# Retention's decays earlier on GpSimd, block-end copies behind the cosine chain, one input split moved

## The chip, the cores and the metric

One core of one Trainium2 chip runs the whole program. The metric is the device time of one execution in microseconds (us); the time before is the median of three runs.

## What is computed

Retention (a linear attention with a decay per head) over 4 batches, 8 heads, 576 positions and 64 channels, then two feed-forward layers of 2304 tokens with 512 inputs and 2048 hidden columns. All inputs are fp32.

```python
scores = scale * np.matmul(q, k.transpose(0, 1, 3, 2))
ret = scores * Dmat          # Dmat[i, j] = gamma[h] ** (i - j) for i >= j, else 0
x = np.matmul(ret, v)        # to [2304, 512]
h = x @ w_in;  g = h * np.cos(h);  x = g @ w_out
h = x @ w_in2; g = piecewise(h);   return g @ w_out2   # 0, (h + 1)**2 / 4 or h
```

## The kernel before, in words

Each fp32 product is made as three TensorE products of a rounded high part and a low remainder (high by high, high by low, low by high). So every activation has a high part (`gh`, made by ScalarE, ACT) and a low part (`gl`, made by GpSimd, POOL, as the difference of the value and its high part).

The first layer runs in "slots", 80 of them. A slot is one pair of a token block (256 tokens once, then four blocks of 512) and one of 16 hidden column groups. Slots 32 to 47, 48 to 63 and 64 to 79 are blocks 2, 3 and 4; the last slots of blocks 0 and 1 are 27 and 31. The program is written out slot by slot (the loop at line 1044), and from slot 24 on every engine keeps the order in which the steps are written. The steps of slot s have letters (line 653): `m` is the first product (12 matmuls into bank `h`, or into `bkS`/`bkO` in block 4), `a` and `A` round the phase (ACT, then DVE), `b` is the cosine (two ACT instructions, `t<-t`), `C` multiplies by h (DVE, `t<-t,h`), `g` and `G` make `gh` and `gl`, and `M` is the second product (12 matmuls into the four banks `bky0` to `bky3`), which is issued two slots later (`LAG`). One slot of the loop from slot 28 on writes, in this order: `C`, `g`, `G` of the slot before; the plan of half slot 2s; `m`; some conversion work; `a`, `A`; the plan of half slot 2s + 1; `M` of slot s - 2; `evac`; conversion work on DVE; `b`; conversion work on ACT.

"Conversion work" turns the second layer's weights, which arrive as 64-bit words, into fp32 pieces (`X`, `W`, `V`, `cw`, `tw`): a queue for DVE and one for ACT, from which the loop takes a budget per half slot (`drain`).

`evac` (line 600) copies the four `bky` banks to SBUF after a block's last second product: ACT takes banks 0 and 2, DVE banks 1 and 3 (`st`), and SyncE (SP) stores them. A block's last second product is issued in slots 29, 33, 49 and 65.

The retention for blocks 3 and 4 runs inside the slots of the block before, in nine chunks (numbers 11 to 19) of 64 or 128 tokens. Function `mk` (line 690) puts each chunk's steps at half slots: the load of q, k, v (`qkv`) at `gl_`, 5 to 9 half slots ahead; the decays on POOL, which multiply q (`qkv<-qkv,qtb`) and, save for a batch's last chunk, k (`qkv<-qkv,ktb`) by powers of gamma; at `pos[0]` the scores and the product with the carried state (TensorE into `bkO` and `bkS`) and the masking (`masked`, DVE, `R`); at `pos[1]` `attend`, the state products and the new state (`T`); at `pos[2]` `high` (ACT) and `low` (DVE), which read `bkO` and `bkS` into the next block's input `xhl`. Chunks 14 and 19 end a batch and have no k decay. The scores of the next chunk use the same two banks, so they also wait for `low`.

The second layer's program comes from a list of operations with positions, which `listed` (line 1318) sorts. Its inputs are split into high and low by `split_q` (line 888): seven splits, of which those in `EARLY` are written at the end of the first layer and the others, with their positions in `XEARLY`, in the list. Each is a copy on ACT (`xc<-q`) and a difference on DVE. The first product of the second layer fills bank `bkT0`; `seed`, an ACT copy `bkT<-bkT`, puts it into `bkT1`, where the next product (of `PRODS` index 2) adds to it.

Nearly all instructions carry line 128, a helper's, so places are told by tile names and times.

Of the kernel before, what the change touches and what calls it, by code (L numbers as in the profile page):

```python
# [23 lines left out]
NC = DFF // P  # L24
# [10 lines left out]
NKB = NQ // 2  # L35
NX = 9
SPOS = (-44, -42)
EARLY = (0, 2, 3, 1, 4)
XEARLY = {5: 6, 6: 8}
T0 = 28.0  # L40
ORDER = "1 5 6 2 7 G 4 3".split()
FIRST = "1 L0 6 L1 2 5 7 N 4 3".split()
# [9 lines left out]
LAG = 2  # L52
# [58 lines left out]
def retention_moe_kernel(ctx: ExitStack, tc: tile.TileContext, qk, kv, win1, wout1, win2, wout2, ktab, out):  # L111
# [25 lines left out]
    V, A, G, SY, PE = [Ordered(e) for e in (nc.vector, nc.scalar, nc.gpsimd, nc.sync, nc.tensor)]  # L137
# [117 lines left out]
    def begin(L, i, c, after=None):  # L255
        return Conversion(L, i, c, after).X()
# [3 lines left out]
    def home1(i, c):  # L260
        if i == 0:
            wi[0, c] = wr.tile([P, 2, DM], F32R, tag="wi", name="wi")
            return wi[0, c]
        wo[0, c] = wp.tile([P, 2, DM], F32R, tag=f"wo{c}", name=f"wo{c}")
        return wo[0, c]

    def store1(c):
        SY.dma_start(out=wd[c], in_=f(wi[0, c]))
# [6 lines left out]
    def load_wi(c):  # L275
        t = wr.tile([P, 2, DM], F32R, tag="wi", name="wi")
        SY.dma_start(out=f(t), in_=wd[c])
        wi[0, c] = t

    xhl = {}  # L280
    CH = {}
# [269 lines left out]
    slots = []  # L551
# [42 lines left out]
    def copy_out(e, t, y, scale):  # L594
        if e % 2 == 0:
            A.activation(t, y, AF.Copy, scale=scale)
        else:
            V.tensor_scalar(out=t, in0=y, scalar1=scale, scalar2=None, op0=ALU.mult)

    def evac(s, home=None, only=None):  # L600
        l, c = slots[s]
        if c != NC - 1:
            return
        o, n = BLOCKS[l]
        per = 512 // n
        for e, y in enumerate(yb[l]):
            if only not in (None, e):
                continue
            t = stp.tile([P, 512], F32, tag="st", name="st") if home is None else home
            copy_out(e, t, y, -TWOPI)  # L610
            SY.dma_start(out=yd[:, e * per:(e + 1) * per, o:o + n], in_=t.rearrange("p (k n) -> p k n", k=per))
# [44 lines left out]
    def steps_of(s, which):  # L656
        for x in which:
            if (x, s) not in taken:
                taken.add((x, s))
                STEPS[x](s)  # L660
# [3 lines left out]
    def at(pos, fn):  # L664
        plan.setdefault(pos, []).append(fn)

    def run_plan(pos):
        for fn in plan.pop(pos, []):
            fn()
# [9 lines left out]
    for l in range(3, NBLK):  # L679
        s0, s1 = window[l]  # L680
        span = 2 * (s1 - s0) / len(members[l])
        for k, i in enumerate(members[l]):
            g = int(2 * s0 + k * span)
            e = int(2 * s0 + (k + 1) * span) - 1
            e = max(e, g)
            pos = [g, g + (e - g) // 3, e]
            ends[i] = e
            gl_ = max(g - 9, ends.get(i - 2, -99))

            def mk(i=i, g=g, pos=pos, gl_=gl_):  # L690
                def ld():
                    CH[i] = Chunk(i)
                    CH[i].place_in()
                    CH[i].load(after=lastpe[0])

                def go(*names):
                    return lambda: [getattr(CH[i], n)() for n in names]
                at(gl_, ld)
                at(g - 1, lambda: CH[i].decay_q(G))
                if not CHUNKS[i][1] + CHUNKS[i][2] == S:  # L700
                    at(g - 1, lambda: CH[i].decay_k(G))
                at(pos[0], go("scores", "across", "masked"))
                at(pos[1], go("attend"))
                if not CHUNKS[i][1] + CHUNKS[i][2] == S:
                    at(pos[1], go("state"))
                at(pos[1], go("add_state"))
                at(pos[2], go("high", "low"))
                crowd[pos[0]] = crowd.get(pos[0], 0.0) + 0.3
                crowd[pos[2]] = crowd.get(pos[2], 0.0) + 0.85
            mk()  # L710
# [146 lines left out]
    def home_early(tag, shape, dt=F32):  # L857
        if not early_pool:
            opening.close()
            early_pool.append(ctx.enter_context(tc.tile_pool(name="ep", bufs=1, side="right", reuse_waits="tile")))  # L860
        return early_pool[0].tile([P, *shape], dt, tag=tag, name=tag)

    def xat(k):
        if k not in xplace:
            if k in EARLY[:2]:
                xplace[k] = home_early(f"xc{k}", (2, 2, TH), F32R)
# [12 lines left out]
    def sum_q(eng, pos, to, a, b, how):  # L879
        e = G if eng == "POOL" else V  # L880

        def run():
            if qa[to][1] is None:
                qa[to][1] = home_early(f"q{to}", (2, TH))
            e.tensor_tensor(out=qa[to][1], in0=qa[a][1], in1=qa[b][1], op=how)
        op(eng, "pool" if eng == "POOL" else "wide", pos, run, (qa[a][0], qa[b][0]), (qa[to][0],))

    def split_q(eng, pos, k, sb=0):
        p = PRODS[k][0]
        if p == 6:  # L890
            sum_q(eng, pos - 2, 0, 4, 0, ALU.subtract)
        if p == 3:
            sum_q(eng, pos - 2, 3, 3, 0, ALU.subtract)
        u = qa[{1: 0, 6: 0, 2: 3, 7: 1, 5: 4, 4: 2, 3: 3}[p]]
        x = (sb * 7 + k) % NX
        hi, lo = ("x", x, 0), ("x", x, 1)
        op("ACT", "copy", pos, lambda: A.activation(xat(x)[:, 0], u[1], AF.Copy), (u[0],), (hi,))
        op("DVE", "wide", pos + 0.8, lambda: V.tensor_tensor(out=xat(x)[:, 1], in0=u[1], in1=f(xat(x)[:, 0]), op=ALU.subtract), (u[0], hi), (lo,))
# [18 lines left out]
    sum_q("DVE", 0, 1, 0, 1, ALU.subtract)  # L917
    for k in EARLY:
        split_q("DVE", 0, k)
# [9 lines left out]
    def drain(eng, budget, most=1e9):  # L929
        q = todo2[eng]  # L930
        while q and (q[0][2] is None or q[0][2] in seen2) and q[0][0] <= budget + 0.15 and (eng != "DVE" or spent[0] < most):
            cost, fn, _, says = q.pop(0)
            fn()
            seen2.add(says)
            budget -= cost
            spent[0] += cost * (eng == "DVE")
# [3 lines left out]
    def raw_of(j):  # L940
        load_raw(1, *bg[j])
# [96 lines left out]
    def then_last():  # L1038
        if not todo2["DVE"] and not todo2["ACT"] and last_work:
            for n, (eng, cost, fn) in enumerate(last_work):  # L1040
                queue_up(eng, cost, fn, ("last", n - 1) if n else None, ("last", n))
            last_work.clear()

    for s in range(N1):
        l, c = slots[s]
        if s == 24:
            by_hand[0] = 0
        if s >= bg0:
            by_hand[0] = 1
            share = whole * (s + 1.5 - bg0) / (N1 - 3 - bg0)  # L1050
            if s == bg0:
                for j in range(3):
                    raw_of(j)
            then_last()
            steps_of(s - 1, "CgG")
            run_plan(2 * s)
            for c2 in reload.get(s, []):
                load_wi(c2)
            steps_of(s, "m")
            drain("ACT", 1.1)  # L1060
            drain("DVE", 2.3 - crowd.get(2 * s, 0.0), share)
            steps_of(s, "aA")
            drain("ACT", 0.65)
            run_plan(2 * s + 1)
            steps_of(s - LAG, "M")
            evac(s - LAG)
            drain("DVE", 1.5 - crowd.get(2 * s + 1, 0.0), share)
            steps_of(s, "b")
            drain("ACT", 0.65)
            if s == N1 - 12:  # L1070
                for _, _, fn in inputs_at:
                    fn()
            continue
        run_plan(2 * s)
        steps_of(s, "m")
        if s >= 1:
            steps_of(s - 1, "CgG")
        steps_of(s, "haA")

        todo = [x for x in jobs.get(s, []) if x not in opened]  # L1080
        begun = [begin(0, *x) for x in todo]
        for x in todo:
            begun.pop(0).rest(home1(*x))
            if queue:
                load_raw(0, *queue.pop(0))
        for x in todo:
            if x[0] == 0:
                store1(x[1])
        run_plan(2 * s + 1)
        if s >= LAG:  # L1090
            steps_of(s - LAG, "M")
            evac(s - LAG)
        steps_of(s, "b")
        for c2 in reload.get(s, []):
            load_wi(c2)
# [211 lines left out]
    for k in range(7):  # L1307
        if k not in EARLY:
            split_q("DVE", XEARLY[k], k)
    for n in range(NSB * NKB):  # L1310
# [150 lines left out]
```

## Time and profile before

| | us |
|---|---|
| median of 3 runs | 846.78 (846.37, 846.78, 851.21) |
| the profiled execution | 849.83 |
| its span, first to last instruction | 848.0 |
| TensorE busy | 814.7 (96%) |
| VectorE (DVE) busy | 642.5 (76%) |
| ScalarE (ACT) busy | 542.3 (64%) |
| GpSimd (POOL) busy | 145.3 (17%) |

The first layer ends near 490 us; the rest is the second layer. In the rows a timeline line gives start, duration, engine, line, operation, what it writes and reads, shapes and count; in brackets the idle time of the engine before it and what ended it. The name there is that of the semaphore which came last by the profile. PE is TensorE.

### The profile page before, as it was taken

To read this page: it belongs to the slowest core of one execution; us is meant where nothing else is said; L and a number is where in the kernel's file an instruction comes from. 1 tells how busy PE (TensorE), PEld (TensorE's weight loads), DVE (VectorE), ACT (ScalarE), POOL (GpSimd) and SP (SyncE) were. 2 spreads that over 40 slices of the span, in tenths; PEclk is the share of its full clock that TensorE was granted. 3 is DMA by queue.
4 is the path that set the end of the run, shared out by engine and by line. 5 is a ranking of instruction groups with operands and counts; after the bars stand their busy time and mean duration, and the time that the engine had idled before them with its cause. 6 is when DMAs were issued, how large, how long until landed. Compare 5 with 4: busy or idle time off the path is not lost.

```text
span 848.0 us, 14727 instructions
## 1 busy us (share of the span) xinstructions
PE 814.7 (96%) x5550; PEld 733.9 (87%) x5550; DVE 642.5 (76%) x941; ACT 542.3 (64%) x889; POOL 145.3 (17%) x115
## 2 busy tenths in 40 slices
PE   8999899978999999999999989999999999999997
PEld 5888788866778777778878889999999999999997
DVE  7888878886678776778877558789597776874776
ACT  4778788745356655556665559778648786566672
POOL 2333222232322332322332100000000000000000
PEclk9999999998999999999999999999999999999999
DMA  9996999688567978666976468988889878898883
GB/s 350 379 385 255 346 329 324 238 287 296 176 246 257 339 277 321 217 219 247 357 295 219 161 214 287 319 255 255 255 292 332 276 255 257 252 325 252 252 254 137
DMA packets 78007, 232.92 MB, mean 275 GB/s; under 512 B 8304, under 2 KB 15088, under 8 KB 77936
## 3 DMA queue, kind: packets, MB, share of 16 engines
q1 hardware_dynamic: 77936, 231.98, 78.6%
q8 instruction: 44, 0.72, 0.3%
q14 instruction: 27, 0.22, 0.1%
HBM read 184.76 MB, written 47.19 MB: 274 GB/s over the span
## 4 chain that ended last, share of the span: by engine, by line
PE 54%; DVE 11%; ACT 6%; DMA 2%; issue 2%; SPq 0%; DVEq 0%; ACTq 0%
PE bkT L128 41%; PE h L128 6%; PE bky L128 5%; ACT t L128 4%; DVE t L128 4%; DVE V L128 3%; DVE tw L128 1%; PE bkO L128 1%; DMA wi<-wd 1%; DVE X L128 1%; PE bkS L128 1%; ACT tw L128 1%; DVE cw L128 1%; DVE xc L128 1%; ACT xc L128 0%
## 5 line engine op out<-in xcount | busy, mean ns | idle before, releaser
L128 PE MATMUL h<-xhl,wi 128*128 128x512 f32 (+1 forms) x816 | 184.3, 376 | 6.0 <-ACT hs L128 2.8
L128 PE MATMUL bkT<-xc,w 128*128 128x384 f32 x1008 | 180.5, 337 | 2.8 <-ACT bkT L128 2.8
L128 PEld LDWEIGHTS bkT<-xc,w 128*128 128x128 f32 x1008 | 176.3, 189 | 3.6 <-ACT bkT L128 3.5
L128 PEld LDWEIGHTS h<-xhl,wi 128*128 128x128 f32 x816 | 144.8, 193 | 34.6 <-ACT hs L128 3.2
L128 PE MATMUL bkT<-gh,w 128*128 128x384 f32 x672 | 170.9, 335 | 0.3 <-ACT bkT L128 0.3
L128 PE MATMUL bky<-gh,wo 128*128 128x512 f32 x504 | 155.5, 395 | 0.0
L128 POOL TENSOR_TENSOR gl<-t,gh 128x512 fp32r<-128x512 f32 (+1 forms) x76 | 101.9, 1341 | 311.2 <-ACT gh L128 244.6
L128 ACT ACTIVATE t<-t 128x512 f32<-128x512 f32 (+1 forms) x152 | 89.4, 591 | 60.4 <-DVE t L128 58.3
L128 PEld LDWEIGHTS bkT<-gh,w 128*128 128x128 f32 x672 | 121.4, 188 | 0.6 <-ACT bkT L128 0.6
L128 PE MATMUL bkT<-gl,w 128*128 128x384 f32 x336 | 112.3, 334 | 0.0
L128 PEld LDWEIGHTS bky<-gh,wo 128*128 128x128 f32 x504 | 94.7, 191 | 19.9 <-issue 0.3
L128 PE MATMUL bky<-gl,wo 128*128 128x512 f32 x252 | 96.0, 391 | 0.0
L128 DVE SCALAR_TENSOR_TENSOR t<-t,h 128x512 f32<-128x512 f32 x88 | 60.1, 683 | 29.4 <-ACT t L128 29.3
L128 ACT ACTIVATE gh<-t 128x512 fp32r<-128x512 f32 (+1 forms) x76 | 44.9, 591 | 33.8 <-DVE t L128 33.7
L128 PEld LDWEIGHTS bkT<-gl,w 128*128 128x128 f32 x336 | 63.1, 188 | 0.0
L128 PEld LDWEIGHTS bky<-gl,wo 128*128 128x128 f32 x252 | 47.6, 189 | 10.2
L128 DVE TENSOR_TENSOR gl<-a,gh 128x768 fp32r<-128x768 f32 x48 | 45.1, 953 | 13.5 <-ACT gh L128 13.5
L128 DVE SCALAR_TENSOR_TENSOR a<-bkT,a 128x768 f32<-128x768 f32 x36 | 34.4, 955 | 23.5 <-ACT a L128 22.9
L128 DVE TENSOR_TENSOR a<-bkT,a 128x768 f32<-128x768 f32 (+1 forms) x46 | 43.0, 937 | 11.0 <-PE bkT L128 11.0
L128 ACT ACTIVATE t<-h 128x512 f32<-128x512 f32 x44 | 26.0, 591 | 38.9 <-PE h L128 38.7
L128 ACT ACTIVATE X<-raw 128x512 f32<-128x512 f32 x61 | 40.4, 664 | 11.4 <-DMA raw<-in_win_dram 7.3
L128 ACT ACTIVATE gh<-a 128x768 fp32r<-128x768 f32 x48 | 40.2, 838 | 9.0 <-PE bkT L128 8.4
(159 smaller groups left out, 1211.5 us busy)
## 6 DMA issues: line engine op xcount, KB each, us to landing
w<-wq SPq DMA_DIRECT2D x84, 512.0 KB, 4.5
w<-wv SPq DMA_DIRECT2D x84, 512.0 KB, 4.4
wi<-wd SPq DMA_DIRECT2D x48, 512.0 KB, 4.7
raw<-in_win_dram SPq DMA_DIRECT2D x32, 512.0 KB, 5.2
raw<-in_wout_dram SPq DMA_DIRECT2D x32, 512.0 KB, 5.2
qkv<-in_qk_dram SPq DMA_DIRECT2D x16, 512.0 KB, 6.4
qkv<-in_kv_dram SPq DMA_DIRECT2D x16, 512.0 KB, 7.9
wd<-wi SPq DMA_DIRECT2D x16, 512.0 KB, 6.0
```

Source lines behind the costliest of these rows:

```text
L128: ins = fn(*args, **kw)
```

## The change

Three edits. The decays of chunks 11 to 19 are written at half slot g - 3 instead of g - 1, where g is the half slot of the chunk's scores. In the slots in which a block's last second product is issued, `C` of the same slot is written directly after `b`, and `evac` after that; the ACT conversion work at the end of such a slot is left to the next one. The split with index 4 (of the fifth product) moves from the first layer's end into the second layer's list, at position 4.

```diff
-EARLY = (0, 2, 3, 1, 4)
-XEARLY = {5: 6, 6: 8}
+EARLY = (0, 2, 3, 1)
+XEARLY = {4: 4, 5: 6, 6: 8}
...
                 at(gl_, ld)
-                at(g - 1, lambda: CH[i].decay_q(G))
+                at(g - 3, lambda: CH[i].decay_q(G))
                 if not CHUNKS[i][1] + CHUNKS[i][2] == S:
-                    at(g - 1, lambda: CH[i].decay_k(G))
+                    at(g - 3, lambda: CH[i].decay_k(G))
...
             steps_of(s - LAG, "M")
-            evac(s - LAG)
             drain("DVE", 1.5 - crowd.get(2 * s + 1, 0.0), share)
             steps_of(s, "b")
-            drain("ACT", 0.65)
+            if slots[s - LAG][1] == NC - 1:
+                steps_of(s, "C")
+                evac(s - LAG)
+            else:
+                drain("ACT", 0.65)
```

On POOL, at the first of the nine places (chunk 11; `gl` of slot 31 is the last of the four before the decays), - is before and + after:

```order
 L651 TENSOR_TENSOR gl<-t,gh 128x512
 L128 TENSOR_TENSOR gl<-t,gh 128x256
-L128 TENSOR_TENSOR gl<-t,gh 128x512 x4
+L128 TENSOR_TENSOR gl<-t,gh 128x512 x3
 L128 TENSOR_TENSOR qkv<-qkv,qtb 128x512
 L128 TENSOR_TENSOR qkv<-qkv,ktb 128x512
```

The two decays now stand ahead of one more `gl`; the same holds for each of the other eight chunks.

On ACT at the end of block 1 (slot 33), before; `t<-h` is step `a`, `t<-t` step `b`, and the two `st` are the copies of banks 0 and 2:

```order
L128 ACTIVATE gh<-t 128x512
L128 ACTIVATE t<-h 128x512
L128 ACTIVATE st<-bky_1077 128x512
L128 ACTIVATE st<-bky_1079 128x512
L128 ACTIVATE t<-t 128x512 x2
L128 ACTIVATE gh<-t 128x512
L128 ACTIVATE tw<-V 128x4x256
```

The same place in the changed kernel:

```order
L128 ACTIVATE gh<-t 128x512
L128 ACTIVATE t<-h 128x512
L128 ACTIVATE t<-t 128x512 x2
L128 ACTIVATE st<-bky_1077 128x512
L128 ACTIVATE st<-bky_1079 128x512
L128 ACTIVATE gh<-t 128x512
L128 ACTIVATE tw<-V 128x4x256
```

The cosine passes the two copies; `gh` stays behind them. On DVE at that place, step `C` (`t<-t,h`) passes the copies of banks 1 and 3:

```order
 L128 SCALAR_TENSOR_TENSOR T<-T,ktb,bkS 128x64 x2
 L128 SCALAR_TENSOR_TENSOR T<-T,ktb,bkO 128x64 x2
+L128 SCALAR_TENSOR_TENSOR t<-t,h 128x512
 L128 TENSOR_SCALAR st<-bky_1078 128x512
 L128 TENSOR_SCALAR st<-bky_1080 128x512
-L128 SCALAR_TENSOR_TENSOR t<-t,h 128x512
 L128 TENSOR_TENSOR tw<-V,tw 128x4x256
 L128 TENSOR_TENSOR V<-W,X 128x512
```

In slots 29, 49 and 65 the same exchange is made, and the conversion copy `X<-raw` of ACT also falls behind `gh`; in slots 49 and 65 the four stores of `st` fall behind one store of converted weights on SP. At the second layer's start ACT issues the same copies with one exchange: the `seed` copy `bkT<-bkT` comes ahead of the second of two `xc<-q` copies instead of behind it. TensorE's order is the same from the first to the last instruction.

## Rows read from the trace of the kernel before

**Rows 1.** Timeline of PE: the instructions before which it sat idle, from 180 us on.
```profile
184.15 0.48 PE L128 MATMUL bkO<-qkv 64*64 64x128 f32 x2 [4.40 <-POOL qkv L128]
...
206.35 0.48 PE L128 MATMUL bkO<-qkv 64*64 64x128 f32 x2 [4.04 <-POOL qkv L128]
...
227.26 0.33 PE L128 MATMUL bkO<-qkv 64*64 64x128 f32 x2 [1.95 <-DVE xhl L128]
...
246.41 0.27 PE L128 MATMUL bkO<-qkv 64*64 64x64 f32 x2 [0.87 <-POOL qkv L128]
...
296.17 0.33 PE L128 MATMUL bkO<-qkv 64*64 64x128 f32 x2 [0.51 <-POOL qkv L128]
...
316.70 0.33 PE L128 MATMUL bkO<-qkv 64*64 64x128 f32 x2 [1.09 <-POOL qkv L128]
...
340.27 0.33 PE L128 MATMUL bkO<-qkv 64*64 64x128 f32 x2 [1.40 <-DMA wi<-wd]
...
361.58 0.33 PE L128 MATMUL bkO<-qkv 64*64 64x128 f32 x2 [1.89 <-POOL qkv L128]
...
428.31 3.00 PE L128 MATMUL h<-xhl,wi 128*128 128x512 f32 x12 [1.45 <-DVE t L128]
...
490.59 3.71 PE L128 MATMUL bkT<-xc,w 128*128 128x384 f32 x12 [2.79 <-ACT bkT L128]
```
**Rows 2.** Timeline of POOL: the decays of chunk 11, and q's of chunk 18.
```profile
182.39 1.71 POOL L128 TENSOR_TENSOR qkv<-qkv,qtb 128x512 f32<-128x512 f32 x1
184.06 1.22 POOL L128 TENSOR_TENSOR qkv<-qkv,ktb 128x512 f32<-128x512 f32 x1
...
338.95 1.27 POOL L128 TENSOR_TENSOR qkv<-qkv,qtb 128x512 f32<-128x512 f32 x1
```
**Rows 3.** Instructions on tile qkv, 200 to 495 us: the landing times of its loads.
```profile
DMA to landing us min/median/max: 3.4/5.3/7.4
```
**Rows 4.** Timeline of DVE around chunks 11 and 12.
```profile
177.84 0.42 DVE L128 TENSOR_SCALAR W<-X 128x512 int32<-128x512 int32 x1
178.29 0.43 DVE L128 TENSOR_SCALAR X<-W 128x512 int32<-128x512 int32 x1
...
183.49 0.89 DVE L128 TENSOR_SCALAR W<-X 128x512 int32<-128x512 int32 x1
184.42 1.15 DVE L128 TENSOR_SCALAR X<-W 128x512 int32<-128x512 int32 x1
...
187.16 0.55 DVE L128 TENSOR_TENSOR R<-bkS,mtb 128x384 f32<-128x384 f32 x1
...
190.40 0.69 DVE L128 SCALAR_TENSOR_TENSOR t<-t,h 128x512 f32<-128x512 f32 x1 [0.21 <-ACT t L128]
...
195.32 0.69 DVE L128 SCALAR_TENSOR_TENSOR t<-t,h 128x512 f32<-128x512 f32 x1 [0.44 <-ACT t L128]
...
203.87 0.41 DVE L128 TENSOR_TENSOR xhl<-bkO,xhl 128x256 fp32r<-128x256 f32 x1
```
**Rows 5.** Timeline of ACT: the end of block 1, and the start of the second layer.
```profile
193.50 0.60 ACT L128 ACTIVATE st<-bky 128x512 f32<-128x512 f32 x1 [0.79 <-PE bky L128]
194.00 1.29 ACT L128 ACTIVATE t<-t 128x512 f32<-128x512 f32 x2
...
488.28 1.56 ACT L128 ACTIVATE xc<-q 128x768 fp32r<-128x768 f32 x2
489.75 0.79 ACT L128 ACTIVATE bkT<-bkT 128x768 f32<-128x768 f32 x1
```
**Rows 6.** Timeline of PE: first products of slots 33, 38 and 60.
```profile
186.07 3.60 PE L128 MATMUL h<-xhl,wi 128*128 128x512 f32 x12
...
228.31 4.59 PE L128 MATMUL h<-xhl,wi 128*128 128x512 f32 x12
...
372.22 2.88 PE L128 MATMUL h<-xhl,wi 128*128 128x512 f32 x12
```
**Rows 7.** Windows: length, busy us (instructions) of PE, PEld, DVE, ACT, POOL, PEclk, DMA share, GB/s.
```profile
200.00:230.00 30.00, 24.01 (x227) 19.08 (x226) 20.20 (x35) 14.25 (x26) 11.47 (x8) 0.86 0.68 241
```

## The prediction, made before the run

> **What bounds the kernel now.** I read the page first: TensorE is busy for 96% of the span, so only its idle time, and time at the lower clock, can be won. Then its timeline, looking for rows with a bracket. From 180 us on there are ten such waits [rows 1]. Eight stand before the scores of a chunk of retention (four 64-row matmuls into `bkO` and `bkS`): chunk 11 at 184.15, 12 at 206.35, 13 at 227.26, 14 at 246.41, 16 at 296.17, 17 at 316.70, 18 at 340.27 and 19 at 361.58. They sum to 4.40 + 4.04 + 1.95 + 0.87 + 0.51 + 1.09 + 1.40 + 1.89 = 16.15 us. Six are put down to POOL's decays. The one at 340.27 names a DMA, but q's decay ended at 338.95 + 1.27 = 340.22, just before it [rows 2], so I count it with them. The one at 227.26 names DVE's `xhl`, the copy of the previous chunk out of the same two banks.
>
> Idle time costs a second time, through the clock. The granted clock was 0.86 between 200 and 230 us [rows 7], and 1.0 is the 2.4 GHz level: (1 - 0.86) x 30 = 4.2 us of work lost, behind the waits of chunks 11 and 12. The first product of slot 38, right behind the wait of chunk 13, took 4.59 us and that of slot 33, behind chunk 11's, 3.60, against 2.88 undisturbed [rows 6]: 1.7 and 0.7 more.
>
> **The decays.** Nine decays of q and seven of k move ahead of one `gl` each. POOL stands idle there: `gl` waits for `gh`, and the decays no longer wait for anything but their loads, which land 3.4 to 7.4 us after their issue [rows 3] and are issued three to six half slots before the new place (a half slot holds at least one product of 2.88 us [rows 6], so over 8 us). So they end before the scores are due, at all nine places, and nothing behind them on POOL is held: a pair takes 1.71 + 1.22 = 2.93 us [rows 2] of a POOL that is busy for 17%. What is late next is another matter, and it differs by chunk.
>
> Chunk 11: the scores can start 4.40 us earlier. But `attend` needs `R`, which DVE ends at 187.16 + 0.55 = 187.71 [rows 4], behind work of its own queue. Today `attend` starts when slot 33's first product ends, at 186.07 + 3.60 = 189.67 [rows 6]. So 2.0 us are won here and the rest is a wait in another place.
>
> Chunk 12: its scores then wait for `low` of chunk 11, which ends at 203.87 + 0.41 = 204.28 [rows 4], 2.07 us before today's start. This end is set by DVE and ACT and not by chunk 11's scores, so the 2.0 of chunk 11 is inside what chunk 12 gains and isn't added. Here the second edit helps. In slot 33 `a`'s rounding ended on DVE at 190.40 + 0.69 = 191.09, but step `C` began only at 195.32 [rows 4], because the cosine (194.00) stood behind copies that waited for `bky` until 193.50 [rows 5]. With the cosine in front, `C` starts at 191.1 + 1.3 = 192.4, which is 2.9 earlier. `gh` still stands behind the second copy (end 194.10 instead of `C`'s end at 196.01), so what follows it is 1.9 earlier. From that I take off 0.7, because chunk 12's decays now run beside these DVE steps: beside chunk 11's, `X` took 1.15 instead of 0.43 us [rows 4]. That leaves 1.2, between 0 and 2.9. Chunk 12's scores: 2.07 + 1.2 = 3.3 us earlier. Of the 4.2 us of clock I take half, 2.1, since a wait of several us remains in front of `attend`. Together 5.4, between 2.0 and 4.40 + 4.04 + 4.2 + 0.7 = 13.3.
>
> Chunk 13: the releaser is `low` and stays. Its DVE chain loses the company of the decays there, and gets it earlier. Between 0 and 1.95; I take 1.0, and half of the 1.7 of clock behind it: 1.9, between 0 and 3.7.
>
> Chunks 14, 16, 17, 18, 19: waits of 0.5 to 1.9 us that end with the decays. The same search for what is late next ends near the old end of TensorE's work there, so I take them whole: 0.87 + 0.51 + 1.09 + 1.40 + 1.89 = 5.8, between 0 and 5.8.
>
> **The price on DVE.** POOL takes as long as before, but DVE meets it at other instructions. Beside chunk 11's decays `W` took 0.89 instead of 0.42 and `X` 1.15 instead of 0.43 [rows 4]: 1.2 us for a pair of 2.93 us. Today this falls into TensorE's waits; moved, it falls into DVE's ordinary work, which has 24% of the span idle as its cover. I take nothing beyond the 0.7 above; without that cover it is 1.2 for each of seven pairs, 8.4. The Trainium skill ("SBUF — State Buffer", section "Who interferes with whom") has a harder rule: a DVE instruction with two SBUF inputs, or in a two-port mode, and a GpSimd instruction that reads SBUF shut each other out, and the second waits until the first ends. By it a pair would cost its whole length, 2.93 or 20.5 for seven uncovered ones, where the rows show 1.2 and so 8.4. That rule speaks against this change, and the third rival below rests on the same rows.
>
> **Block ends.** Besides the gain counted at chunk 12, the four copies of a block come later by at most the cosine and `C`, 1.29 + 0.69 = 2.0 us [rows 4, 5]. The next block's first `M` needs those banks, but the first product of a slot, 2.88 us [rows 6], lies between. Cost: 0 to 2.0 at each of slots 34, 50 and 66; I take 0. At slot 66, where DVE runs late, a delay is likeliest; the wait of 1.45 at 428.31 [rows 1] would give most of it back. The stores of the copies on SP leave a little later, and their reader is the second layer.
>
> **The split.** At 490.59 TensorE waits 2.79 us for `seed` [rows 1]. It starts at 489.75, behind two `xc` copies of 1.56 together [rows 5]; now it is behind one: 0.7 earlier, between 0 and 0.8. The copy that falls behind it feeds the fifth product; three products lie between.
>
> **The sum.** 5.4 + 1.9 + 5.8 + 0.7 = 13.8 us. Behind 372 us TensorE's order is full anyway, and the second layer starts when the first ends, so all of it arrives at the end. The profiled execution took 849.83, so 836.0. It was itself 3.05 slower than the median of 846.78; I suppose that its surplus lies in such waits, so I don't take 13.8 from the median as well. The predicted time is 836.0, which is 10.8 below the median; its own range is 831 to 841.
>
> **Rivals.** First, the waits only move: TensorE waits for `R` or `low` at most chunks instead of for the decays. For it speaks that `xhl` already is the releaser once; against it, that `low` of chunk 11 ended 2.07 before the scores of 12. Then half of the 5.8 and the split are left, 3.6 us, and from the median that is 843. Second, all goes, the clock too: 16.15 + 4.2 + 1.7 + 0.7 + 0.7 = 23.5, and 849.83 - 23.5 = 826. Against it stands `R` of chunk 11. Third, slower: the decays shut DVE out for their whole length, in the stretch that makes `C`, `gh` and `R`. Seven pairs of 2.93 and two single ones of 1.3 are 23.1 us; less the 13.8 won, 9.3 more than the median, 856. It decides from the point at which DVE has no idle time left ahead of `C`; the stretch of 1.2 in a pair speaks against it.
>
> **How the numbers follow.** A measurement of this kernel can tell about 1% (8.5 us) from no change, so faster means below 838.3. Chances: the forecast 0.62, the moved waits 0.23, all gone 0.10, slower 0.05. Of the forecast's own range a small part, 0.06, lies above 838.3. Faster: 0.62 + 0.10 - 0.06 = 0.66. Within 1%: 0.23 + 0.06 + 0.01 = 0.30. Slower: 0.04. The range of 8 in 10 goes from 828, near the second rival, to 843, the first.
>
> **What would show it.** Right: no wait for `qkv` before any scores; a wait of some 4 us before chunk 11's `attend`, ended by DVE's `R`; chunk 12's scores 3 us earlier against the span's start; the granted clock from 200 to 230 us above 0.9; `seed` 0.7 closer behind the product before it. Wrong: waits before scores that name `xhl` and are as long as today's; DVE's `W`, `X`, `V`, `tw` stretched ahead of `C` while POOL works; a wait before the first `M` of a block, at slots 34, 50 or 66.

## The result, and the profile after

The changed kernel took 836.0 us (median of four runs, 835.64 to 837.64) against 846.58 for the kernel before in the same session (four runs, 845.5 to 851.21). The ratio is 0.9868, with a 95% interval of 0.983 to 0.9907: 10.6 us or 1.3% faster. Over all the comparisons below, the kernel before spread from 844.87 to 851.74. One execution of experiment 1 ran at a granted clock of 0.85 and took 890.2 us; no number below uses it.

The profiled execution of the changed kernel took 836.01, so it stands on its median; that of the kernel before (849.83) stood 3.05 above its own. The page's span and totals:

```profile
span 834.2 us, 14726 instructions
...
PE 809.7 (97%) x5549; PEld 729.7 (87%) x5550; DVE 644.7 (77%) x941; ACT 541.6 (65%) x889; POOL 146.4 (18%) x115
```

The work of the engines is what it was. What changed are TensorE's waits. The timeline of PE in the changed kernel, at the places of [rows 1] and three new ones (177.37, 183.98, 394.33):

```profile
177.37 3.03 PE L128 MATMUL h<-xhl,wi 128*128 128x512 f32 x12 [0.75 <-DVE t L128]
...
183.98 0.32 PE L128 MATMUL bkS<-R,qkv 64*64 64x128 f32 x1 [3.58 <-DVE R L128]
...
199.45 0.33 PE L128 MATMUL bkO<-qkv 64*64 64x128 f32 x2 [1.24 <-DVE xhl L128]
...
218.01 0.33 PE L128 MATMUL bkO<-qkv 64*64 64x128 f32 x2 [1.84 <-DVE xhl L128]
...
219.06 3.02 PE L128 MATMUL h<-xhl,wi 128*128 128x512 f32 x12
...
234.75 0.27 PE L128 MATMUL bkO<-qkv 64*64 64x64 f32 x2
...
303.99 0.33 PE L128 MATMUL bkO<-qkv 64*64 64x128 f32 x2 [0.62 <-DVE xhl L128]
...
326.15 0.33 PE L128 MATMUL bkO<-qkv 64*64 64x128 f32 x2
...
347.10 0.33 PE L128 MATMUL bkO<-qkv 64*64 64x128 f32 x2 [1.53 <-DVE xhl L128]
...
394.33 0.74 PE L128 MATMUL bky<-gh,wo 128*128 128x512 f32 x2 [1.08 <-ACT st L128]
...
469.13 2.35 PE L128 MATMUL bkT<-xc,w 128*128 128x384 f32 x12 [0.70 <-DVE t L128]
...
476.78 2.98 PE L128 MATMUL bkT<-xc,w 128*128 128x384 f32 x12 [2.56 <-ACT bkT L128]
```

No row names POOL's `qkv` any more. Chunk 11's 4.40 has become a wait of 3.58 one step later, ahead of `attend` (183.98). The product between, slot 33's first, has one of 0.75 ahead of it, which goes with the opening (below). Chunks 14 and 18 (234.75, 326.15) have no wait left. Chunks 12, 13, 17 and 19 wait for `xhl`, the previous chunk's `low`: 1.24, 1.84, 0.62 and 1.53, where they had 4.04, 1.95, 1.09 and 1.89. New are 1.08 at slot 66, ended by a block-end copy, and 0.70 ahead of the second layer's first product.

The granted clock, by windows of the changed kernel (columns as in [rows 7]):

```profile
200.00:230.00 30.00, 28.16 (x311) 22.80 (x301) 24.80 (x44) 14.42 (x25) 8.93 (x7) 1.00 0.72 259
...
175.00:190.00 15.00, 10.67 (x140) 8.39 (x139) 13.88 (x25) 8.96 (x17) 3.52 (x3) 0.89 0.76 253
```

From 200 to 230 it is 1.00 where it was 0.86. What is left at half speed lies behind the wait of 3.58: (1 - 0.89) x 15 = 1.65 us. Slot 38's first product (219.06) took 3.02 instead of the 4.59 of [rows 6].

**Where the difference lies.** Starts of the same TensorE instruction in the two profiled executions can be subtracted, since its order is the same from end to end. The first such difference is in a part that the change doesn't touch: slot 28's first product, behind the whole opening. Timeline of PE and the window 80 to 100 us, kernel before:

```profile
91.95 2.93 PE L128 MATMUL h<-xhl,wi 128*128 128x256 f32 x12 [2.48 <-ACT hs L128]
...
153.62 2.68 PE L128 MATMUL h<-xhl,wi 128*128 128x512 f32 x11
```

```profile
80.00:100.00 20.00, 17.19 (x94) 15.12 (x93) 17.13 (x36) 16.59 (x36) 2.81 (x3) 0.91 0.87 328
```

The same for the changed kernel:

```profile
89.10 1.70 PE L128 MATMUL h<-xhl,wi 128*128 128x256 f32 x12 [1.74 <-ACT hs L128]
...
149.30 2.91 PE L128 MATMUL h<-xhl,wi 128*128 128x512 f32 x12
```

```profile
80.00:100.00 20.00, 18.26 (x113) 16.32 (x112) 16.66 (x32) 15.90 (x36) 5.50 (x5) 1.00 0.96 348
```

Here 153.62 - 149.30 = 4.32 us lie between them already, 1.8 of it in the half-speed stretch behind the longer wait ((1 - 0.91) x 20). In the ten profiled executions whose distances or waits stand here, all with the same opening, slot 28 starts between 149.00 and 153.62; the kernel before was caught at the late end. So of the spans' 848.0 - 834.2 = 13.8 us, 9.5 lie in the stretch of the change. From here on the 4.32 are taken off. What is won by each place, then (start before, start after, difference less 4.32, step):

| place | before | after | won so far | step |
|---|---|---|---|---|
| `attend` of chunk 11 | 189.60 | 183.98 | 1.3 | 1.3 |
| scores of chunk 12 | 206.35 | 199.45 | 2.6 | 1.3 |
| first product of slot 36 | 214.11 | 204.97 | 4.8 | 2.2 |
| first product of slot 38, its end | 232.90 | 222.08 | 6.5 | 1.7 |
| scores of chunk 14 | 246.41 | 234.75 | 7.3 | 0.8 |
| scores of chunk 17 (with 16) | 316.70 | 303.99 | 8.4 | 1.1 |
| scores of chunk 18 | 340.27 | 326.15 | 9.8 | 1.4 |
| scores of chunk 19 | 361.58 | 347.10 | 10.2 | 0.4 |
| slot 70's first product | 428.31 | 413.75 | 10.2 | 0.1 |
| second product of layer 2 | 490.59 | 476.78 | 9.5 | -0.7 |

Between chunk 19 and slot 70 some 1.5 were lost at slot 66 and won back.

The first step is smaller than what the change won there. DVE does not share all of the 4.32: its `tw` ahead of chunk 11's scores starts 21.44 us behind slot 28 in the kernel before (at 175.06), and 22.13 in the changed kernel (at 171.43). Experiment 5 below runs the changed kernel's order up to slot 65; there slot 28 starts at 151.68 and `tw` 21.35 behind it. Its timeline of PE, `attend` of chunk 11:

```profile
185.56 0.32 PE L128 MATMUL bkS<-R,qkv 64*64 64x128 f32 x1 [3.60 <-DVE R L128]
```

That is 33.88 behind slot 28, against 34.68 in the changed kernel and 35.98 before, and the wait of 0.75 ahead of slot 33's first product is missing. It stands (0.73 to 0.75) in the changed kernel and experiments 6 to 8, whose slot 28 starts at 149.00 to 150.14, and not in experiments 1, 4 and 5, where it starts at 150.75 to 152.37. So about 0.7 of the 4.32 is lost again at this place, and with openings alike the change is worth some 10.2 us instead of 9.5. Read from experiment 5, it has won 2.1 at `attend`, 3.4 at chunk 12's scores and 5.6 at slot 36.

### The profile page after: what moved, and what is told of

The parts are those of the page before. It is cut to its first block, busy times and chain, and to the rows that moved or that the text cites. A ratio compares the mean times of both kernels' runs of the same rounds, so it can differ in the third digit from the quotient of the medians.

```text
span 834.2 us, 14726 instructions
## 1 busy us (share of the span) xinstructions
PE 809.7 (97%) x5549; PEld 729.7 (87%) x5550; DVE 644.7 (77%) x941; ACT 541.6 (65%) x889; POOL 146.4 (18%) x115
## 4 chain that ended last, share of the span: by engine, by line
PE 63%; DVE 12%; ACT 6%; DMA 2%; issue 1%; SPq 0%; DVEq 0%; ACTq 0%
PE bkT L128 41%; PE bky L128 10%; PE h L128 7%; DVE V L128 3%; DVE t L128 3%; ACT t L128 2%; PE bkS L128 2%; PE bkO L128 2%; DVE X L128 1%; DVE tw L128 1%; DVE cw L128 1%; ACT tw L128 1%; DVE xc L128 1%; DVE W L128 0%; ACT gh L128 0%
## 5 line engine op out<-in xcount | busy, mean ns | idle before, releaser
L128 PE MATMUL h<-xhl,wi 128*128 128x512 f32 (+1 forms) x816 | 180.6, 371 | 3.1 <-ACT hs L128 1.7
L128 PEld LDWEIGHTS h<-xhl,wi 128*128 128x128 f32 x816 | 142.0, 189 | 30.6 <-ACT hs L128 1.9
L128 PEld LDWEIGHTS bky<-gl,wo 128*128 128x128 f32 x252 | 47.8, 190 | 10.2
```

What stands on the lines that cost most here:

```text
L128: ins = fn(*args, **kw)
```

## The experiments

The ratios are against the kernel before, run on the same chip. Distances are from slot 28's first product to the second product of layer 2, so that most of the opening's luck drops out: 336.97 for the kernel before, 327.48 for the changed one.

**1. The decays alone**, in the kernel before.

```diff
-                at(g - 1, lambda: CH[i].decay_q(G))
+                at(g - 3, lambda: CH[i].decay_q(G))
...
-                    at(g - 1, lambda: CH[i].decay_k(G))
+                    at(g - 3, lambda: CH[i].decay_k(G))
```

> The kernel before with the decays three half slots ahead and nothing else. Theory A (the decays were what TensorE waited for, and only part of each wait comes back because of low and R): 838 to 841 us, no wait for qkv before any scores, a wait of 2 to 4 us before chunk 11's attend ended by R, a wait of 2 us or more before chunk 12's scores ended by xhl (longer than the 1.24 of the changed kernel, because step C of slot 33 is still late), the wait of 1.45 us in slot 70 still there. Theory B (the difference between the two profiles is mostly one of the opening, and the decays only move waits): 843 to 847.

Measured: 840.99 (median of three), ratio 0.9912 (0.9895 to 0.9929), so 0.9% of the change's 1.3%. The same kernel ran once more, for its trace.

> The decays alone once more, for a profile. Theory A: as for the run with the decays alone: no wait for qkv; before chunk 12's scores a wait of 2 us or more for xhl; step C of slot 33 ends some 6 us after that slot's first product although the decays are gone, because the cosine still stands behind the block's copies. Theory A' (after the copies alone halved chunk 12's wait, the chain from the block's end is common to both edits): chunk 12's scores wait about 2.0 us here.

Measured: 842.43, distance 330.89. Timelines of PE and of DVE in this kernel:

```profile
186.32 0.47 PE L128 MATMUL bkS<-R,qkv 64*64 64x128 f32 x1 [3.59 <-DVE R L128]
...
203.78 0.48 PE L128 MATMUL bkO<-qkv 64*64 64x128 f32 x2 [3.30 <-DVE xhl L128]
...
483.26 3.88 PE L128 MATMUL bkT<-xc,w 128*128 128x384 f32 x12 [3.29 <-ACT bkT L128]
```

```profile
188.66 0.68 DVE L128 SCALAR_TENSOR_TENSOR t<-t,h 128x512 f32<-128x512 f32 x1
...
193.50 0.69 DVE L128 SCALAR_TENSOR_TENSOR t<-t,h 128x512 f32<-128x512 f32 x1 [0.44 <-ACT t L128]
```

The decays alone turn chunk 11's wait into one for `R`, as in the changed kernel. Chunk 12 then waits 3.30 for `low`, 2.06 more than with the copies moved (1.24). Step `C` of slot 33 (193.50) stands 4.84 behind the rounding step `A` (188.66), as it did before the change (195.32 - 190.40 = 4.92 in [rows 4]). The whole change, DVE's timeline at the same place:

```profile
186.31 0.68 DVE L128 SCALAR_TENSOR_TENSOR t<-t,h 128x512 f32<-128x512 f32 x1
...
188.35 0.69 DVE L128 SCALAR_TENSOR_TENSOR t<-t,h 128x512 f32<-128x512 f32 x1 [0.59 <-ACT t L128]
```

Here it is 2.04: `C` no longer waits for the block's copies. So the second edit does what it says, at chunk 12's scores, and its size there is 2.06. Chunk 17, behind the copies of slot 49, gains too: its wait is 1.36 with the decays alone and 0.62 in the changed kernel. One sign that was expected did not come: slot 70's wait is not 1.45 here but 0.71, named after the load of a weight tile.

**2. The copies alone**, in the kernel before.

```diff
-            evac(s - LAG)
...
-            drain("ACT", 0.65)
+            if slots[s - LAG][1] == NC - 1:
+                steps_of(s, "C")
+                evac(s - LAG)
+            else:
+                drain("ACT", 0.65)
```

> The kernel before with only the block-end copies behind the cosine and step C. Theory A (the decays carry the gain; the copies only help chunk 12 once the decays are gone): 845 to 847 us, step C of slot 33 some 3 us earlier against A of slot 33, but chunk 12's scores still wait about 4 us for the decays; a wait of about 1 us before the first second product of block 4 (slot 66), given back at slot 70. Theory B (the copies shorten the chain that sets the end): 841 to 843.

Measured: 846.72, ratio 0.9978 (0.9957 to 0.9999), distance 336.11. Timeline of PE:

```profile
202.81 0.33 PE L128 MATMUL bkO<-qkv 64*64 64x128 f32 x2 [2.01 <-POOL qkv L128]
...
405.02 0.73 PE L128 MATMUL bky<-gh,wo 128*128 128x512 f32 x2 [1.09 <-ACT st L128]
...
488.21 4.21 PE L128 MATMUL bkT<-xc,w 128*128 128x384 f32 x12 [3.30 <-ACT bkT L128]
```

Chunk 12's wait halves, 4.04 to 2.01, though its decays have not moved. The decays stand behind a `gl`, that `gl` waits for `gh`, and `gh` for `C`, so an earlier `C` brings them forward too. Chunk 17's wait of 1.09 is gone here as well. The block-end wait at slot 66 is there as in the changed kernel (1.09 here, 1.08 there), so it comes with the copies' new place.

**3. The split alone**, in the kernel before.

```diff
-EARLY = (0, 2, 3, 1, 4)
-XEARLY = {5: 6, 6: 8}
+EARLY = (0, 2, 3, 1)
+XEARLY = {4: 4, 5: 6, 6: 8}
```

> The kernel before with only the split of index 4 moved. Theory A (it takes one ACT copy of 0.7 us from in front of seed): the wait before the second product of the second layer goes from 2.79 to 2.1 us, 845.5 to 846.5 us in all. Theory B (the step before seed on DVE and ACT sets its time): wait unchanged at 2.8, 846.6.

Measured: 846.91, ratio 0.9986 (0.9967 to 1.0006): by the time alone it can't be told from nothing. Timeline of PE, the second product of layer 2:

```profile
487.45 3.92 PE L128 MATMUL bkT<-xc,w 128*128 128x384 f32 x12 [2.48 <-ACT bkT L128]
```

The wait fell by 2.79 - 2.48 = 0.31. The distance did not fall: it is 337.55, 0.58 more than before. This execution's opening ended early (slot 28 at 149.90), and chunk 11's scores waited 4.93 instead of 4.40. The three parts sum to 0.88 + 0.22 + 0.14 = 1.24% by the times, the whole is 1.32%; each has an interval of 0.2% or more either way, so they add up as far as this can be told. By the distances they are 6.1 + 0.9 - 0.6 = 6.4 of 9.5 us.

**4. The decays' own price**, in the changed kernel.

```diff
-                at(g - 3, lambda: CH[i].decay_q(G))
-                if not CHUNKS[i][1] + CHUNKS[i][2] == S:
-                    at(g - 3, lambda: CH[i].decay_k(G))
+                pass
```

> The changed kernel with the decays of chunks 11 to 19 left out (nine of q, seven of k; all other work as before). Theory A (where they stand now the decays are hidden, and cost only their stretch of a few DVE instructions, 1.2 us a pair, of which most lies in idle time): 832 to 836 us, and the waits for R before chunk 11's attend and for xhl before the scores of chunks 12, 13, 17 and 19 stay, each shorter by at most 1.2. Theory C (POOL shuts DVE out for the length of each pair, 2.93 us, on the chain that makes low and R): 822 to 828, those waits gone.

Measured: 831.58, ratio 0.9804 (0.9787 to 0.9821), 4.4 us below the changed kernel; distance 321.55, 5.9 below, of which 0.7 is the opening's. It is just under theory A's range and far above theory C's. Timelines of PE and DVE:

```profile
183.66 0.32 PE L128 MATMUL bkS<-R,qkv 64*64 64x128 f32 x1 [2.78 <-DVE R L128]
...
215.50 0.33 PE L128 MATMUL bkO<-qkv 64*64 64x128 f32 x2 [0.83 <-PE bky L128]
...
342.55 0.33 PE L128 MATMUL bkO<-qkv 64*64 64x128 f32 x2 [0.35 <-PE h L128]
```

```profile
173.66 0.69 DVE L128 TENSOR_TENSOR V<-W,X 128x512 f32<-128x512 f32 x1
...
174.87 0.42 DVE L128 TENSOR_SCALAR W<-X 128x512 int32<-128x512 int32 x1
```

The wait for `R` is still there without any decay, 2.78 of 3.58, so it belongs to DVE's own queue. But chunk 13's wait falls from 1.84 to 0.83, chunk 19's from 1.53 to 0.35, neither named after `xhl` any more, and those of chunks 12 and 17 all but vanish. The cause shows in two views of the changed kernel, POOL's timeline and DVE's, at the decays of chunk 11 and, in the last line of each, of chunk 13:

```profile
171.83 2.29 POOL L128 TENSOR_TENSOR qkv<-qkv,qtb 128x512 f32<-128x512 f32 x1
174.07 1.49 POOL L128 TENSOR_TENSOR qkv<-qkv,ktb 128x512 f32<-128x512 f32 x1
...
205.68 1.29 POOL L128 TENSOR_TENSOR qkv<-qkv,qtb 128x512 f32<-128x512 f32 x1
```

```profile
171.43 1.52 DVE L128 TENSOR_TENSOR tw<-V,tw 128x1024 fp32r<-128x1024 f32 x1 [1.65 <-ACT tw L128]
172.98 1.68 DVE L128 TENSOR_TENSOR V<-W,X 128x512 f32<-128x512 f32 x1
174.58 0.68 DVE L128 SCALAR_TENSOR_TENSOR t<-t,h 128x512 f32<-128x512 f32 x1
175.18 0.67 DVE L128 TENSOR_SCALAR W<-X 128x512 int32<-128x512 int32 x1
...
205.84 1.41 DVE L128 TENSOR_SCALAR W<-X 128x512 int32<-128x512 int32 x1
```

Beside the decays `V` takes 1.68 instead of 0.69 and `W` 0.67 instead of 0.42: 1.24 us more for one pair, near the 1.2 that the prediction had read from other instructions. The start times tell how it comes about:

- `tw` was running when q's decay started at 171.83, and keeps its 1.52 (1.53 without decays). The decay ends at 174.12, 1.17 behind `tw`; alone it takes 1.27 [rows 2].
- `V` starts inside the decay and ends at 174.66, 0.54 behind the decay's end; alone it takes 0.69.
- At chunk 13 q's decay starts first and keeps 1.29. `W` starts inside it, takes 1.41 and ends 0.28 behind it; alone it takes 0.42.
- `t` (174.58), which reads `h` in its bank, runs inside k's decay and keeps its 0.68.

So of these pairs the one that starts second is held until about the end of the first, and its recorded time includes that. For DVE this is no longer hidden: without the decays the waits for `low` shrink.

**5. The last block's copies in their old place**, in the changed kernel.

```diff
             steps_of(s - LAG, "M")
+            if slots[s - LAG] == (3, NC - 1):
+                evac(s - LAG)
...
-            if slots[s - LAG][1] == NC - 1:
+            if slots[s - LAG] == (3, NC - 1):
+                pass
+            elif slots[s - LAG][1] == NC - 1:
...
-            else:
+            if slots[s - LAG][1] != NC - 1 or slots[s - LAG] == (3, NC - 1):
```

> The changed kernel, but with block 3's copies (slot 65) in front of the cosine and step C as before. Theory A (the wait of 1.08 us before the first second product of block 4, and 0.5 behind it, is given back, since DVE's work sets the end of the first layer): 835 to 837, the wait in slot 66 gone, one of about as much before slot 70 or at the end. Theory D (that wait is a plain loss): 834 to 835.

Measured: 835.0 (834.85 to 839.4), ratio 0.9852 (0.9813 to 0.9891). This does not settle it: the intervals of this kernel and the changed one overlap. Timeline of PE:

```profile
414.54 3.00 PE L128 MATMUL h<-xhl,wi 128*128 128x512 f32 x12 [0.61 <-DMA wi<-wd]
```

The wait at slot 66 is gone, and one of 0.61 is back at slot 70, named after the load of a weight tile. In the kernel before 1.45 stood there [rows 1]; in the changed kernel there was none. The distance is 325.51, 2.0 less than the changed kernel's, but 0.8 of that lie ahead of slot 65, where the two kernels are the same. Of the rest 1.5 was won at slot 66, 0.7 lost again by slot 70, and 0.4 won at the second layer's start, where the first product's wait is shorter. The medians differ by 1.0. So in this pair half of the wait is given back at slot 70, and whether the other half reaches the time stays open. The trade is not a fixed one: in experiment 4 both waits stand, 1.11 at slot 66 and 1.35 at slot 70, and with the copies in their old place slot 70's wait was 1.45, 0.71 and 0.88 in the kernel before and in experiments 1 and 3.

**6. `low` half a slot earlier**, in the changed kernel.

```diff
-                at(pos[2], go("high", "low"))
+                at(pos[2] - 1, go("high", "low"))
...
-                crowd[pos[2]] = crowd.get(pos[2], 0.0) + 0.85
+                crowd[pos[2] - 1] = crowd.get(pos[2] - 1, 0.0) + 0.85
```

> The changed kernel with high and low of each chunk one half slot earlier. Theory A (what is left before the scores is the wait for xhl: 1.24 + 1.84 + 0.62 + 1.53 = 5.2 us, and a half slot is longer than each of them): those four waits gone, 830 to 833 us. Theory E (DVE is full there, and low only changes places with steps that TensorE waits for next): 835 to 837.

Measured: 832.86 (832.7 to 833.75), ratio 0.9816 (0.9785 to 0.9847), distance 324.23. Timeline of PE:

```profile
202.54 0.32 PE L128 MATMUL bkS<-R,qkv 64*64 64x128 f32 x1 [0.32 <-DVE R L128]
...
236.29 0.27 PE L128 MATMUL bkS<-R,qkv 64*64 64x64 f32 x1 [0.94 <-DVE R L128]
...
302.73 0.33 PE L128 MATMUL bkO<-qkv 64*64 64x128 f32 x2 [1.04 <-DVE xhl L128]
```

The waits before the scores of chunks 12, 13 and 19 are gone; chunk 17's has grown to 1.04, and short ones for `R` have come (0.32, 0.94, and 0.44 in chunk 18). The net is 3.1 us by the medians and 3.3 by the distances. So most of what the moved decays left behind was a matter of DVE's order, and could be had.

**7. Two more splits behind `seed`**, in the changed kernel.

```diff
-EARLY = (0, 2, 3, 1)
-XEARLY = {4: 4, 5: 6, 6: 8}
+EARLY = (0, 2)
+XEARLY = {3: 1, 1: 3, 4: 4, 5: 6, 6: 8}
```

> The changed kernel with two more splits (index 3 and 1) taken out of the first layer's end into the second layer's list. Theory F (the splits stand in the chain from step C over gh to the next step A in slots 76 to 79, and one ACT copy still stands in front of seed): the wait of 0.70 before the first product of the second layer gone, the one before the second 0.8 shorter or more, 833.5 to 835 us. Theory G (their DVE work comes late in the second layer's start and TensorE waits there): 836 to 838.

Measured: 836.58 (832.28 to 838.31), ratio 0.9848 (0.9798 to 0.9897): inconclusive. Timeline of PE:

```profile
220.18 0.33 PE L128 MATMUL bkO<-qkv 64*64 64x128 f32 x2 [1.95 <-DVE xhl L128]
...
472.94 2.35 PE L128 MATMUL bkT<-xc,w 128*128 128x384 f32 x12 [0.33 <-DVE t L128]
...
478.96 2.35 PE L128 MATMUL bkT<-xc,w 128*128 128x384 f32 x12 [0.94 <-ACT bkT L128]
```

At the end the two waits fell from 0.70 + 2.56 to 0.33 + 0.94, and the product's matmuls from 2.98 to 2.35. (Experiment 5 has 2.36 behind a wait of 2.57, so this last gain need not be the splits'.) But this execution lost about 3 us between 184 and 226 us, where the edit changes nothing: a wait of 1.95 for chunk 13, and the lower clock behind it. One execution of the four came at 832.28.

**8. The edits of 5, 6 and 7 together**, in the changed kernel.

> The changed kernel with low one half slot earlier, block 3's copies in the old order, and splits 3 and 1 in the second layer's list. Theory A (each takes away a different wait of TensorE: 3.1 us for low and 1.0 for the copies by the medians, 1.6 for the wait before the second product by the profiles): 829 to 831. Theory E (DVE's work sets the first layer's end, so they overlap): 832 to 834.

Measured: 828.75 (827.88 to 829.98, five runs), ratio 0.9767 (0.9747 to 0.9788), distance 321.22. It beats both kernels, and its median lies just under theory A's range. Timeline of PE:

```profile
470.22 2.35 PE L128 MATMUL bkT<-xc,w 128*128 128x384 f32 x12 [0.94 <-ACT bkT L128]
```

The gains do not overlap: 836.0 - 828.75 = 7.3 by the medians, which were taken on different chips, and 327.48 - 321.22 = 6.3 by the distances. Experiment 6 has 3.1 and 3.3 of them; the remaining 3.0 to 4.1 go with the edits of 5 and 7 together, whose shares no run separates. The largest wait left is the one for `R` in chunk 11 (3.59).

## Why the prediction was right, and where its sizes were off

The time forecast (836.0) was met, by a sum whose terms were not all right; that it was met to the tenth is luck. Two of its signs of being wrong came in part: DVE's `V` and `W` stretched while POOL works, and a wait at slot 66. Term by term, in us, measured as steps of the table above:

| term | predicted | measured |
|---|---|---|
| chunks 11 and 12, with clock | 5.4 | 4.8 |
| chunk 13, with clock | 1.9 | 1.7 |
| chunks 14, 16, 17, 18, 19 | 5.8 | 3.7 |
| block ends | 0 | about 0 |
| the split, end of layer 1 | 0.7 | -0.7 |
| sum | 13.8 | 9.5 |

(The table's entries are rounded; 9.5 is 13.81 - 4.32. With experiment 5's opening the first row is 5.6.)

**Chunks 11 and 12: right, step by step.** The wait of "some 4 us before chunk 11's `attend`, ended by DVE's `R`" came as 3.58. `attend` won 1.3 where 2.0 were forecast, chunk 12's scores 2.6 where it was 3.3, and the clock behind it 2.2 where it was 2.1. In experiment 5's execution, whose opening is nearer to that of the kernel before, the first two are 2.1 and 3.4. For the copies 1.2 net had been taken, between 0 and 2.9; the pair of kernels with and without them gives 2.06. The decays' stretch of DVE costs more than the 0.7 taken off: without decays the waits for `R` and `low` are 0.8 and 1.2 shorter. One slip is in the sum: of the 4.2 of clock, (1 - 0.71) x 2.8 = 0.8 lie from 227.2 to 230 us, where the granted clock was 0.71, behind chunk 13's wait, and stand in the 1.7 as well. As half of each was taken, 0.4 of the 13.8 is counted twice.

**Chunk 13: right in sum, wrong in its parts.** The wait was to fall by 1.0 and fell by 0.1 (1.95 to 1.84). But the lower clock behind it went altogether, 1.57 on one product (4.59 to 3.02), where half of 1.7 was taken.

**Chunks 14 to 19: the step that failed.** The prediction said that "The same search for what is late next ends near the old end of TensorE's work there, so I take them whole". It holds at 14 and 18, where nothing is waited for any more, and at 16. At chunks 17 and 19 `low` of the previous chunk ended later than that: waits of 0.62 and 1.53 remain, of 1.09 and 1.89. At chunk 17 not even this gain is the decays': alone they leave 1.36, and the copies take it to 0.62. This is the first rival's mechanism, in part: the wait moved from `qkv` to `xhl`. A search that ends "near" an end must be given with its row, for each chunk.

**The price on DVE: mis-sized, and the rule behind it misread.** The prediction took "nothing beyond the 0.7", on the ground that 24% of DVE's span is idle. The decays cost 4.4 us in the kernel as a whole by the medians, and 5.2 by the distances less the opening's 0.7 (experiment 4). DVE's idle time is an average; before `low` and `R` there is little. The bound of 8.4 took 1.2 for each pair: it is 1.24 at chunks 11 and 12, 1.71 at chunk 13 (0.99 on `W`, 0.72 on `X`), and nothing at chunk 18, whose decays meet no instruction that they hold.

The third rival, in which DVE is shut out for a decay's whole length, is refuted in its size (2.93 a pair), not in its mechanism. DVE's instruction is held, but only for what is left of the decay when it starts, and a decay that starts second is held itself. The prediction set 1.2 from its rows against a rule by which the second waits until the first ends; the same rows show that rule. In [rows 2] q's decay ends at 184.10 and k's at 185.28; in [rows 4] `W`, started at 183.49, ends at 184.38, and `X`, started at 184.42, at 185.57, each 0.3 behind the decay that it met; alone they take 0.42 and 0.43. The Trainium skill ("SBUF — State Buffer", section "Who interferes with whom") has it that whichever of the two issues first keeps the shared ports for the whole instruction and the other is blocked until then. This trace agrees: in experiment 4's rows `tw` kept 1.52, the decay ended 1.17 behind it, and `V` 0.54 behind the decay. What a DVE instruction pays depends on where in the decay it starts: `W` at 205.84, 0.16 behind the decay's start, pays 0.99 of 1.29.

**Block ends: within the range.** 0 to 2.0 was given with slot 66 as the likeliest place and slot 70 as where it would be given back. The wait of 1.08 came at slot 66, slot 70's 1.45 went, and experiments 2 and 5 tie the first to the copies. That the one gives back the other shows in the changed kernel and not in experiment 4. Whether it costs up to 1 us in all the runs leave open. What the prediction left out is the copies' gain at chunk 17.

**The split: the gain was there, its place was not.** Alone it shortened the wait by 0.31; in the changed kernel it is 0.23 shorter than before the change, but 0.7 shorter than in experiments 1 and 2 (3.29 and 3.30), which have one of the other edits each and the split in its old place. That fits the 0.7 of the forecast. But 0.70 appeared ahead of the first product, which waits for DVE's last `t`. Timelines of DVE and ACT in the changed kernel, at that end:

```profile
473.94 0.69 DVE L128 SCALAR_TENSOR_TENSOR t<-t,bkO 128x512 f32<-128x512 f32 x1 [1.36 <-ACT t L128]
```

```profile
474.67 0.63 ACT L128 ACTIVATE gh<-t 128x512 fp32r<-128x512 f32 x1 [0.75 <-DVE t L128]
475.20 0.83 ACT L128 ACTIVATE xc<-q 128x768 fp32r<-128x768 f32 x1
475.94 0.79 ACT L128 ACTIVATE bkT<-bkT 128x768 f32<-128x768 f32 x1
```

`seed` stands behind one `xc` copy now, as the change says. But the chain `C`, `gh`, `xc`, `seed` begins at 473.94, and `C` there waits for ACT's cosine. From the `C` before to this one ACT and DVE take 5.55 us (468.39 to 473.94), as in the kernel before (481.46 to 487.02), and 3.92 in experiment 7 (472.20 to 476.12), where no split stands between the two. So these steps and the splits among them set the pace, and TensorE, which comes to them earlier now, waits. Experiments 7 and 8 move two more `xc` copies out of the chain and shorten both waits, which bears this out.

**The profiled execution's surplus: wrong.** "I suppose that its surplus lies in such waits" put 3.05 us into the stretch of the change. The opening, which varies by itself, held 4.32 instead, of which some 0.7 came back at slot 33. So the 13.8 agrees with the difference of the two spans only through the opening. The predicted time was still right because the sum was taken from the profiled execution and came to 10.8 off the median, where 10.6 were measured. The terms as measured, 9.5, or some 10.2 with openings alike, would have given 836.6 to 837.3 from the median. The 13.8 was too large by some 3.6: 2.1 at chunks 14 to 19, and 1.4 at the split and the first layer's end.

## What to carry to other kernels

The length of a wait is an upper bound for what its removal gives. For every place look up the row of what is late next; here 16.15 us of waits and 5.8 of clock (4.2 + 1.7 + 0.7, less the 0.8 counted twice) gave some 10 in all. An engine that is idle for a quarter of the span may have no idle time in front of the one result that is waited for, so price what stretches it at that place. When two instructions stretch each other, compare their starts and ends before giving the stretch a size: here the second was held by the first. Before two profiles are subtracted, find the difference in the part that both share, take it off, and see whether every engine shares it.

## What was not expected of the hardware

The same opening, in ten executions, took between 149.00 and 153.62 us; the waits ended by `hs` and the half-speed stretch near 90 us differ from one to the next.

Waits of nearly the same length were followed by the lower clock or not: 1.95 before chunk 13 was (kernel before, and experiment 7), 1.84 before chunk 13 (changed kernel) and 1.89 before chunk 19 (kernel before) were not. Ahead of the second layer's second product, 2.56 was followed by a granted clock of 0.76 from 476 to 483 us (changed kernel), and 2.57 by 1.00 from 477 to 484 (experiment 5). Behind the first of the waits before chunk 13, one product took 1.57 us more than in the changed kernel. What decides between them was not tried.

When a decay on POOL and an instruction like `V`, `W`, `X` or `tw` on DVE overlap, the one that started first keeps its time and the other is held: `tw` 1.52 and then the decay 2.29 instead of 1.27, the decay 1.29 and then `W` 1.41 instead of 0.42. An instruction between the two can be held and hold: `V` waits for q's decay, and k's decay, which starts inside `V`, takes 1.49 instead of 1.03 (chunk 18, where it meets none).
